# A weight's conversion in the token stage: the last addition done by an accumulating DMA inside SBUF instead of VectorE

## The chip, the cores and the metric

The kernel runs on one core of one Trainium2 chip. The metric is the device time of one execution in microseconds (us). A core has a matmul engine (TensorE, "PE" in the profile; "PEld" is its weight loads), three engines for elementwise work (VectorE "DVE", ScalarE "ACT", GpSimd "POOL") and 16 DMA engines. Each engine works through its instructions in order. DMAs are issued from the instruction streams of SyncE ("SP"), ACT or POOL; those of SP and ACT go through a hardware queue (q1 and q10 in the profile), those of POOL through a software queue (q0), for which POOL itself spends time on each issue.

## What is computed

Hashed attention on 4 x 8 heads, 768 tokens, head width 64; its output, as 4 batches of 768 tokens by 512 columns, goes through a token mixer and a channel mixer:

```python
xt = x.transpose(0, 2, 1)
h = np.maximum(xt @ w_tok1, 0.0) @ w_tok2          # 768 -> 256 -> 768, over tokens
u = x + h.transpose(0, 2, 1)
h2 = np.maximum(u @ w_ch1, 0.0) @ w_ch2            # 512 -> 1536 -> 512, over columns
return (u + h2).astype(np.float32)
```

The four weights arrive in float64 (a float32 array multiplied by a float64 scalar). The kernel sees each number as two 32-bit words, the low and the high one, and turns it into float32 on the chip. The weight of this case is `w_ch2`, 1536 x 512, "second channel weight" below.

## The kernel before

The kernel has three stages, and the order of the instructions on every engine is the order in which the program emits them. **Attention** (0 to about 297 us) keeps its result transposed in the tile `XT`, 4 blocks of 128 columns by 3072 tokens. The **token stage** (`tokens`, about 297 to 368 us) follows, then the **channel stage** (`channels`).

*The token stage.* For each batch b, `mix1(b)` multiplies `w_tok1` with the batch (24 matmuls of 512 columns in two output halves j, L1226), and ScalarE applies the relu (L1233) into `r1`. `left_sums(b)` makes four sums of `r1` on VectorE (L1249 to L1252), and `mix2(b, m)`, for the two halves m, does the second product by seven smaller matmul products instead of eight (L1266). Their results lie in four PSUM banks; ScalarE copies some out (`p1` first, L1271, then L1274, L1276, L1278), VectorE adds them up (L1281 to L1285) into one of three `places` (parts of the tile `second`, used in rotation: `(2*b + m + 1) % 3`), and an accumulating DMA issued from POOL (L1286) adds that place to `XT`. There are eight of these DMAs, two per batch. A `mix2` may write its place only when the DMA that read the place three turns earlier has landed. All PSUM results of the stage share eight banks in rotation. The order is: `mix1(0)`, the sums of the token weight (`weight_sums`, L1203 to L1206), `left_sums(0)`; then for b = 1, 2, 3: `mix1(b)`, `left_sums(b)`, `mix2(b-1, 0)`, `mix2(b-1, 1)`; at the end `mix2(3, 0)`, the first inputs of the channel stage (`inputs`, L1178 and L1179), `mix2(3, 1)`.

*The conversions.* Between these, at fixed places, `job()` takes the next entry of a list: first the sums of the first channel weight (L1316 to L1321), then eight times `conversion.one`, each for a piece of `w_ch2` of 128 partitions x 3 row blocks x 256 columns (768 numbers per partition). Calls of `job` stand after each half of `mix1` and between the two `mix2` of b = 1, 2, 3. So conversion 1 comes at the end of `mix1(0)`, conversions 2 and 3 in `mix1(1)`, 4 between `mix2(0, 0)` and `mix2(0, 1)`, 5 and 6 in `mix1(2)`, 7 between `mix2(1, 0)` and `mix2(1, 1)`, 8 in `mix1(3)`; `mix2(2, .)` and `mix2(3, .)` have none left.

`one` consists of four steps. `begin` lets ScalarE write |high word as float32| x 2^-112 into `size` (L177). `join` works on VectorE: L187 makes `unit`, the power of two that the number's exponent stands for, by shifting `size` and masking; L191 shifts `size` in place, which gives the absolute value cut to the bits of the high word; L195 multiplies the low word by 2^-52 and by `unit`; L196 adds this to `size`. `end` (L206, VectorE) puts the sign of the high word on the sum and writes it into `WC2`, the float32 weight. `fetch` (L169, SP) loads the next raw piece. `size` has two buffers, `raw` three, and `unit` one.

Of the kernel before, what the change touches and what calls it, by code (L numbers as in the profile page):

```python
# [36 lines left out]
F32 = mybir.dt.float32  # L37
BF16 = mybir.dt.bfloat16
U32 = mybir.dt.uint32
I32 = mybir.dt.int32  # L40
I64 = mybir.dt.int64
ALU = mybir.AluOpType
# [6 lines left out]
def kernel(  # L49
# [16 lines left out]
    nc = tc.nc  # L66
    P = 128
# [9 lines left out]
    NHT = DCH // P  # L77
# [56 lines left out]
    NW = 768  # L134
# [6 lines left out]
    class Conversion:  # L141


        def __init__(self, pool, parts, bufs):
            self.pool, self.bufs = pool, bufs
            self.todo = [
                (w, dst, rows, j, n)
                for w, dst, rows, blocks in parts
                for j in range(*blocks, rows)
                for n in range(0, dst.shape[2], NW // rows)  # L150
            ]
            self.fetched, self.begun, self.ready = [], None, None
            for _ in range(bufs - 1):
                self.fetch()
# [55 lines left out]
        def turnover(self):  # L210

            self.end()
            self.fetch()

        def one(self):

            self.begin()
            self.join()
            self.end()
            self.fetch()  # L220
# [1085 lines left out]
    def weight_sums(w, sums, first, second, low, high):  # L1306

        a00, a01 = w[:, first, low], w[:, second, low]
        a10, a11 = w[:, first, high], w[:, second, high]

        def early():
            nc.vector.tensor_tensor(sums[:, 1], a00, a10, op=ALU.subtract)  # L1316
            nc.vector.tensor_tensor(a10, a10, a11, op=ALU.add)

        def late():
            nc.vector.tensor_tensor(sums[:, 0], a10, a00, op=ALU.subtract)  # L1320
            nc.vector.tensor_tensor(sums[:, 2], a01, sums[:, 0], op=ALU.subtract)  # L1321

        return [early, late]

    def channels(pool, psum, SW1, second, TA, judge):
# [384 lines left out]
        def hidden_pair(s, t):  # L1710
# [5 lines left out]
            r, (p2, p6, p7, p3, p4) = parts_of(s, t)  # L1716
            p5, p1 = Smaller(None, "p5", s, t), ahead.pop()
            one, two, three, four = ring
            e2, e4, e5, e3 = [flat(output_at(i)) for i in ((2, 1, 1, 2) if t == 1 else (0, 1, 3, 2))]
            e6 = e7 = flat(q1)  # L1720
# [52 lines left out]
            p3.rest()  # L1773
            p3.unite()
            A = bank_pair(one)
            p4.one(A, e4)
            p7.seed()
# [23 lines left out]
            if t + 1 < GP:  # L1801
                later(t + 1, "p3", *bounds(r))
                later(t + 1, "end", lambda: relu(r[3]), lambda: relu(r[2]))
                open_next(two, s, t)
                if t == 1:
                    end_look()
                ring[:] = [two, three, one, four]
                postponed.append((direct, end))
            else:
                plus(r[1], banks(C), rows(e3))  # L1810
                unfinished.append(lambda: (relu(r[3]), [work() for work in bounds(r)]))
                ring[:] = [two, one, three, four]
                postponed.append((direct, lambda: (end(), relu(r[2]))))
# [402 lines left out]
    def inside(stage, *args):  # L2216
        with tc.tile_pool(name="sb", bufs=2, reuse_waits="tile") as pool, tc.tile_pool(
            name="ps", bufs=2, space=PSUM, reuse_waits="tile"
        ) as psum, tc.manual_schedule():
            stage(pool, psum, *args)  # L2220
# [10 lines left out]
    n = NHT // 4 * P  # L2231
# [10 lines left out]
    def attention_and_tokens(W1, W2, x0):  # L2242
        inside(attention, W1, W2, x0)
        pool = late.enter_context(tc.tile_pool(name="late", bufs=1, side="right", reuse_waits="tile"))
        SW1 = big["SW1"] = pool.tile([P, 3, NCB // 2, DCH // 2], F32, name="SW1")
        TA = big["TA"] = pool.tile([P, 2, NCB // 2, TT], F32, name="TA")
        n = NHT * DM

        def second_tile(i):
            return pool.tile([P, (n, n * 3 // 4)[i]], F32, name=f"second{i}", tag=f"second{i}", bufs=1)  # L2250

        WC2 = second["WC2"] = second_tile(0).rearrange("p (k c) -> p k c", k=NHT)
        second["SW2"] = second_tile(1).rearrange("p (i k c) -> p i k c", i=3, k=NHT // 2)
        second["tile"] = second_tile

        def weights(pool):
            return Conversion(pool, [(w_ch2, WC2, 3, (0, NHT))], bufs=3)

        def jobs(conversion):
            early, late = weight_sums(  # L2260
                WC1, SW1, slice(0, NCB // 2), slice(NCB // 2, NCB), slice(0, DCH // 2), slice(DCH // 2, DCH),
            )
            return [
                lambda: (early(), late()),
                *[conversion.one] * (NHT * DM // NW),
            ]

        SW2 = second["SW2"].rearrange("p i k c -> p i (k c)")
        places = [SW2[:, i] for i in range(3)]
        inside(tokens, W1, W2, x0, weights, jobs, [TA[:, 0], None, TA[:, 1], None], places)  # L2270
# [100 lines left out]
```

## Time and profile before

| | |
|---|---|
| runs shown | 766.54, 766.83, 766.92 us, median 766.83 |
| profiled execution | span 766.2 us from the first to the last instruction; its own execution time is not listed apart from the three runs |
| PE busy | 758.5 us, 99% of the span |
| DVE busy | 673.5 us, 88% |
| ACT, POOL busy | 442.4 us (58%), 189.7 us (25%) |
| accumulating DMAs of the token stage (L1286) | 8, of 768 KB each |
| pieces of `w_ch2` converted | 8, of 384 KB (float32) each |

In the profile, a group line reads: line, engine, operation, output<-input tiles, shapes, count | busy us, mean ns of one | idle time of the engine before them and what ended it. A timeline line reads: start in us, duration in us, engine, line, operation, tiles, count, and in brackets the idle time before it with its releaser; "<-issue" stands for a wait whose cause the profile doesn't show. `WC2` and the three `places` appear under the tile name `second`, `r1` as `r`, the token weights as `W`, PSUM banks of the stage as `t`. A line of a view by stretches gives the stretch in us, its length, then the busy time of each engine with its number of instructions, the granted TensorE clock, the busy share of the DMA engines and GB/s. The lines themselves stand in the prediction.

### The profile page before, as it was taken

The numbers are of one execution on the slowest core, as the hardware profiler recorded it, in microseconds if no ns is written. First come the engines' busy times: TensorE is split into PE (matmuls) and PEld (weight loads), VectorE is DVE, ScalarE is ACT, GpSimd is POOL, SyncE is SP. The second block draws the span as 40 slices with busy tenths as digits, with TensorE's granted clock in tenths as the row PEclk, the third lists the DMA queues.
The fourth block names the chain that finished last, engine by engine and source line by source line (L and its number), as shares of the span: only waits on it lengthen the run. The fifth ranks groups of instructions, "written<-read, shape, count | busy, mean of one in ns | idle before, by whom it ended". The sixth has DMA issues, their size and how long they took to land.

```text
span 766.2 us, 14575 instructions
## 1 busy us (share of the span) xinstructions
PE 758.5 (99%) x5549; PEld 509.8 (67%) x5549; DVE 673.5 (88%) x969; ACT 442.4 (58%) x816; POOL 189.7 (25%) x266
## 2 busy tenths in 40 slices
PE   9999999999999999999999999999999999999997
PEld 4565655666656554455444468888877888886886
DVE  5899899899997998999788798998899799889884
ACT  6677777677776873333232326566666667665331
POOL 2346771638761820011220100100000011000001
PEclk9999999999999999999999999999999999999999
DMA  7746587575965549876697997889576696750665
GB/s 257 271 172 184 179 240 225 181 179 186 217 202 116 168 68 254 310 178 119 112 321 244 348 360 263 244 233 277 171 220 210 234 261 140 235 157 8 207 157 130
DMA packets 131210, 157.80 MB, mean 206 GB/s; under 512 B 56000, under 2 KB 99520, under 8 KB 129216
## 3 DMA queue, kind: packets, MB, share of 16 engines
q1 hardware_dynamic: 119248, 136.05, 56.3%
q0 software_dynamic: 11600, 20.53, 13.1%
q8 instruction: 45, 0.74, 0.4%
q10 hardware_dynamic: 288, 0.25, 0.1%
q14 instruction: 29, 0.24, 0.1%
HBM read 107.71 MB, written 40.67 MB: 194 GB/s over the span
## 4 chain that ended last, share of the span: by engine, by line
PE 88%; DVE 8%; DMA 2%; issue 1%; SPq 0%; DVEq 0%; ACT 0%; ACTq 0%
PE b L1353 51%; PE sc L503 16%; PE acc L470 14%; PE sc L425 1%; PE hash L536 1%; PE ss L848 1%; DVE size L196 1%; PE sacc L874 1%; DVE unit L195 1%; DMA XT<-second 1%; DVE second L206 1%; PE hash L348 1%; DVE size L191 1%; PE ssums L862 1%; PE hash L353 1%
## 5 line engine op out<-in xcount | busy, mean ns | idle before, releaser
L414 ACT ACTIVATE exps<-sc 128x768 f32<-128x768 f32 (+1 forms) x181 | 126.5, 765 | 10.1 <-PE sc L503 7.2
L1353 PE MATMUL b<-R,second 128*128 128x256 f32 (+1 forms) x522 | 131.8, 408 | 0.0
L503 PE MATMUL sc<-qk 32*128 32x384 f32 (+1 forms) x1352 | 120.1, 457 | 0.0
L1353 PEld LDWEIGHTS b<-R,second 128*128 128x128 f32 x522 | 99.1, 190 | 28.5 <-issue 16.5
L470 PE MATMUL acc<-exps,vn 128*32 128x385 f32 (+1 forms) x1344 | 111.7, 486 | 0.0
L503 PEld LDWEIGHTS sc<-qk 32*128 32x128 f32 x1352 | 92.3, 185 | 16.9 <-issue 4.4
L1359 ACT COPY c<-b 128x256 f32<-128x256 f32 (+1 forms) x96 | 40.3, 426 | 79.3 <-PE b L1353 66.1
L470 PEld LDWEIGHTS acc<-exps,vn 128*32 128x32 f32 x1344 | 43.9, 109 | 62.0 <-issue 60.0
L376 POOL DMA_DIRECT2D bits<-XT x104 | 54.6, 526 | 72.1 <-DVE XT L366 27.4
L459 DVE TENSOR_TENSOR esd<-esd,exps 128x768 f32<-128x768 f32 x70 | 67.0, 957 | 4.3
L1353 PE MATMUL b<-XT,WC 128*128 128x256 f32 (+1 forms) x208 | 61.0, 428 | 0.0
L791 POOL DMA_INDIRECT table<-XT,sorting x48 | 57.1, 1190 | 14.7 <-issue 13.2
L2063 POOL DMA_DIRECT2D out<-second x7 | 8.5, 1213 | 187.3 <-DVE second L2057 81.5
L557 ACT COPY rec<-rec 32x384 f32<-32x384 f32 x56 | 28.5, 510 | 41.0 <-DVE rec L551 39.6
L1353 PEld LDWEIGHTS b<-XT,WC 128*128 128x128 f32 x208 | 39.5, 190 | 15.4 <-issue 10.3
L503 PE MATMUL sc<-bits 32*128 32x384 bf16 (+1 forms) x338 | 48.0, 311 | 0.0
L1353 PE MATMUL b<-XT,SW 128*128 128x256 f32 (+1 forms) x164 | 47.0, 410 | 0.0
L455 DVE TENSOR_TENSOR esd<-esd,exps 128x768 f32<-128x768 f32 x42 | 40.3, 958 | 4.4
L1226 PE MATMUL t<-x,W 128*128 128x512 f32 x96 | 42.1, 594 | 0.2 <-DMA x<-bounced 0.2
L1353 PEld LDWEIGHTS b<-XT,SW 128*128 128x128 f32 x164 | 31.1, 190 | 9.4 <-issue 4.1
L1286 POOL DMA_DIRECT2D XT<-second x8 | 9.9, 1233 | 95.8 <-DVE unit L187 56.2
L1226 PEld LDWEIGHTS t<-x,W 128*128 128x128 f32 x96 | 18.1, 190 | 23.3 <-issue 21.7
(333 smaller groups left out, 1455.9 us busy)
## 6 DMA issues: line engine op xcount, KB each, us to landing
second<-left SPq DMA_DIRECT2D x20, 768.0 KB
qk<-in_qk_rows SPq DMA_DIRECT2D x13, 1152.0 KB
raw<-in_moe_w_ch SPq DMA_DIRECT2D x16, 768.0 KB
second<-left SPq DMA_DIRECT2D x18, 576.0 KB
WC<-hidden_left SPq DMA_DIRECT2D x18, 448.0 KB
x<-bounced SPq DMA_DIRECT2D x4, 1536.0 KB
XT<-second POOLq DMA_DIRECT2D x8, 768.0 KB
seen<-in_qk SPq DMA_DIRECT2D x15, 384.0 KB
```

The source lines that it names most:

```text
L376: nc.gpsimd.dma_start(out=to[at : at + 2 * BITS, half[j]], in_=g[of : of + 2 * BITS])
L414: return nc.scalar.activation(e[:, :, columns], sc, ACT.Exp, scale=SCALE)
L455: nc.vector.tensor_tensor(self.d, self.d, e, op=ALU.add)
L459: nc.vector.tensor_tensor(self.d, self.d, e, op=ALU.add)
L470: made = nc.tensor.matmul(acc[D * i + d : D * i + d + 32], vn[:, i, c, d : d + 32], e[:, i], start=(c == 0), stop=(c == NR - 1),)
L503: nc.tensor.matmul(made[j, piece][:, i], k[at : at + 32, ks], q[at : at + 32], start=part < 0, stop=part == 1,)
L557: nc.scalar.copy(rec[other : other + 32, h], rec[at : at + 32, h])
L791: nc.gpsimd.indirect_dma_start(out=tables[2 * w + i], out_offset=bass.IndirectOffsetOnAxis(ap=self.at[:, x : x + 1], axis=0), in_=row, in_ ...
L1226: nc.tensor.matmul(ps, W1[:, r, P * j : P * j + P], x[:, r], start=(r == 0), stop=(r == NR - 1),)
L1286: nc.gpsimd.dma_start(out=XT[:, 2 * m : 2 * m + 2, S * b : S * b + S], in_=to.rearrange("p i n t -> p i (n t)"), accum_op=ALU.add,)
L1353: nc.tensor.matmul(ps, left(k), right(k), start=start and k == ks[0], stop=stop and k == ks[-1], skip_group_check=True,)
L1359: nc.scalar.copy(c, ps)
```

## The change

For the second channel weight alone, `one` calls a new step `signed` between `begin` and `join`; `join` and `end` then find nothing to do. `signed` shifts `size`, puts the sign of the high word on it and writes this into `WC2` directly (the high part of the number, with its sign); takes sign and exponent of that value with the mask 0xFF800000 into `unit`; multiplies the low word by 2^-52 and by `unit` (the low part, with its sign); and adds `unit` to `WC2` by a DMA issued from POOL that accumulates at its destination. Four VectorE instructions and one DMA stand in the place of five VectorE instructions. `unit` keeps its single buffer. The sum is the same; the rest of the kernel, and the conversions of the other three weights, stay as they are.

```diff
-        def __init__(self, pool, parts, bufs):
-            self.pool, self.bufs = pool, bufs
+        def __init__(self, pool, parts, bufs, summed=False):
+            self.pool, self.bufs, self.summed = pool, bufs, summed
...
+        def signed(self):
+
+            raw, size, to, rows = self.begun
+            self.begun = None
+            unit = self.pool.tile([P, NW], F32, name="unit", tag="unit", bufs=1)
+            lo, hi, size, part = (
+                a.rearrange("p (t n) -> p t n", t=rows) for a in (raw[:, :, 0], raw[:, :, 1], size.bitcast(U32), unit)
+            )
+            bits = to.bitcast(U32)
+            nc.vector.tensor_scalar(size, size, 3, None, op0=ALU.logical_shift_left)
+            nc.vector.scalar_tensor_tensor(
+                bits, hi, 0x80000000, size, op0=ALU.bitwise_and, op1=ALU.bitwise_or,
+            )
+            nc.vector.tensor_scalar(part.bitcast(U32), bits, 0xFF800000, None, op0=ALU.bitwise_and)
+            nc.vector.scalar_tensor_tensor(part, lo, 2.0**-52, part, op0=ALU.mult, op1=ALU.mult)
+            nc.gpsimd.dma_start(out=to, in_=part, accum_op=ALU.add)
+
         def one(self):
 
             self.begin()
+            if self.summed and self.begun:
+                self.signed()
             self.join()
             self.end()
             self.fetch()
...
-            return Conversion(pool, [(w_ch2, WC2, 3, (0, NHT))], bufs=3)
+            return Conversion(pool, [(w_ch2, WC2, 3, (0, NHT))], bufs=3, summed=True)
```

## The prediction

> **What bounds the kernel now.** I read the page's first part, then the stretches of the token stage, where the eight conversions lie, then the timelines of POOL, DVE and ACT there.
>
> ```profile
> span 766.2 us, 14575 instructions
> PE 758.5 (99%) x5549; PEld 509.8 (67%) x5549; DVE 673.5 (88%) x969; ACT 442.4 (58%) x816; POOL 189.7 (25%) x266
> ```
>
> ```profile
> core 0: us, PE busy (x) PEld busy (x) DVE busy (x) ACT busy (x) POOL busy (x), PEclk, DMA share, GB/s
> 310.00:320.00 10.00, 10.00 (x31) 5.45 (x30) 9.69 (x16) 5.74 (x11) 0.00 (x0) 1.00 0.77 281
> 330.00:340.00 10.00, 10.00 (x32) 5.79 (x31) 9.69 (x15) 5.94 (x11) 1.27 (x1) 1.00 0.96 200
> 350.00:360.00 10.00, 10.00 (x33) 5.89 (x32) 9.48 (x18) 4.33 (x10) 2.42 (x2) 1.00 0.44 79
> 360.00:370.00 10.00, 9.91 (x30) 5.30 (x29) 9.24 (x16) 3.15 (x7) 1.22 (x1) 1.00 0.76 135
> ```
>
> DVE is nearly full (9.2 to 9.7 of 10), but PE is full: 10.00 of 10.00. DVE lags behind PE and the PSUM banks absorb the lag. So DVE time freed here buys nothing by itself; all of PE's idle time in these rows is the 0.09 us in the last. The end of the kernel moves only if PE is made to wait. The place where PE is nearest to waiting is the last `mix2`:
>
> ```profile
> 365.07 0.48 ACT L1271 COPY second<-t 128x384 f32<-128x384 f32 x1 [2.91 <-DMA XT<-second]
> 365.60 0.30 PEld L1266 LDWEIGHTS t<-W2sums,r1s 128*128 128x128 f32 x2 [0.70 <-ACT second L1271]
> ```
>
> ACT waits 2.91 us there for an accumulating DMA that still reads the place `mix2(3, 1)` wants, and the PE side for ACT. With three places in rotation that is the DMA of `mix2(2, 0)`, the fifth of eight. POOL's timeline shows how they follow each other:
>
> ```profile
> 324.99 1.35 POOL L1286 DMA_DIRECT2D XT<-second  x1 [50.63 <-DVE unit L187]
> 332.61 1.27 POOL L1286 DMA_DIRECT2D XT<-second  x1 [6.27 <-ACT second L1274]
> 343.68 1.20 POOL L1286 DMA_DIRECT2D XT<-second  x1 [9.79 <-DVE second L1285]
> 350.46 1.22 POOL L1286 DMA_DIRECT2D XT<-second  x1 [5.58 <-DVE unit L187]
> 358.57 1.20 POOL L1286 DMA_DIRECT2D XT<-second  x1 [6.89 <-DVE second L1285]
> 365.30 1.22 POOL L1286 DMA_DIRECT2D XT<-second  x1 [5.53 <-issue]
> 372.05 1.20 POOL L1286 DMA_DIRECT2D XT<-second  x1 [5.53 <-DVE TB L1183]
> 378.80 1.21 POOL L1286 DMA_DIRECT2D XT<-second  x1 [5.55 <-DVE seen L1859]
> ```
>
> The last four start 6.73, 6.75 and 6.75 us apart, each after 5.5 us of idle POOL, under three different named releasers, none of which the DMA's data needs. The fifth landed at 365.07 (ACT's wait ends) and POOL starts the sixth at 365.30. I read this as: of DMAs this large, POOL's queue has one in flight, and the next issue waits until it has landed. Small ones do go out closely:
>
> ```profile
> 62.47 1.27 POOL L791 DMA_INDIRECT table<-XT,sorting  x1 [0.38 <-issue]
> 63.74 0.53 POOL L376 DMA_DIRECT2D bits<-XT  x1
> ```
>
> So it is room for descriptors rather than a rule of one at a time. By the code an `XT` DMA has 256 pieces (128 partitions x 2 runs of 3 KB). The new one has 384 (128 x 3 runs of 1 KB at its destination). If two of 256 don't fit together, 256 beside 384 don't either.
>
> **The change part by part.** VectorE's part, from the groups of DVE in the token stage:
>
> ```profile
> L206 DVE SCALAR_TENSOR_TENSOR second<-raw,size 128x768 uint32<-128x768 uint32 x8 | 7.7, 958 | 0.3
> L196 DVE TENSOR_TENSOR size<-size,unit 128x768 f32<-128x768 f32 x8 | 7.7, 958 | 0.3
> L195 DVE SCALAR_TENSOR_TENSOR unit<-raw,unit 128x768 f32<-128x768 uint32 x8 | 7.6, 951 | 0.0
> L191 DVE TENSOR_SCALAR size<-size 128x768 uint32<-128x768 uint32 x8 | 4.5, 560 | 0.3
> L187 DVE TENSOR_SCALAR unit<-size 128x768 uint32<-128x768 uint32 x8 | 4.4, 552 | 0.0
> ```
>
> `signed` keeps one shift (as L191), one sign step (as L206), one mask (as L187) and one multiply (as L195) and drops L196: 8 x 0.96 = 7.7 us of DVE, hidden behind PE. One conversion falls from 3.9 us to 2.95 us: 1.55 to the end of the sign step, 1.4 for the mask and the multiply.
>
> What is added is eight DMAs of 384 KB on POOL's queue. No accumulating DMA of this shape is in the trace, so I build its cycle (issue to next possible issue) from the one that is:
>
> ```profile
> q0 software_dynamic: 272, 0.79, 65.6%
> XT<-second POOLq DMA_DIRECT2D x8, 768.0 KB
> 508.03 0.61 POOL L2170 DMA_DIRECT2D seen<-in_qk  x1 [6.09 <-ACT seen L2160]
> ```
>
> The first line is the DMA queues' view of 365.30 to 372.05 us, when this queue alone ran: 65.6% of 6.75 = 4.4 us of data. Issue takes 1.2 us, and 1.15 us are left for start and landing. For the new DMA: data by bytes 2.2 us; start and landing 1.15; issue 1.8, since 128 pieces take 0.61 us (last line; the 128 from the code) and 256 take 1.2. Together C = 5.2 us. From below it costs half of the row, 3.4 us, if pieces cost nothing at issue and all else goes by bytes. From above, if small pieces move slowly:
>
> ```profile
> q0 software_dynamic: 207, 0.42, 45.1%
> ```
>
> This is 492 to 498 us, a DMA in 2 KB pieces (beside other traffic): 45.1% of 6 us x 16 engines / 207 = 0.21 us a piece, against 0.26 us for 3 KB (65.6% of 6.75 x 16 / 272). On that line 1 KB costs 0.16 us; times 24 per engine, 3.8 us of data, C = 6.8. I take 5.2: of the two rows the first, an accumulation inside SBUF without other traffic, is the nearer.
>
> The Trainium skill ("DMA: Bandwidth & Descriptors", section "Anatomy of one DMA — SWDGE (gpsimd) path") puts a POOL-issued DMA at about 2.0 us plus its bytes at 436 GB/s; an estimate by it is 2.9 us for the new DMA. For the `XT` DMA it gives 3.8 us, where this trace has 6.5 (358.57 to 365.07), so the trace does not agree for accumulating ones. By the page's C the delay worked out below would be about 5 us in place of 21.
>
> Two new waits come with it. First, the `XT` DMAs queue behind the new ones on POOL, and the `places` behind them. Second, `unit` has one buffer: the mask of conversion n+1 on DVE waits until DMA n has landed, and behind it on DVE wait `left_sums` and the additions of `mix2`, which free PSUM banks and feed PE. Now the schedule, with M = 6.73 for an `XT` DMA (landing 0.2 us before the next issue, as above; C likewise), from these starts on DVE:
>
> ```profile
> 304.48 0.56 DVE L187 TENSOR_SCALAR unit<-size 128x768 uint32<-128x768 uint32 x1
> 308.47 0.55 DVE L1203 TENSOR_TENSOR W2sums<-W 128x384 f32<-128x384 f32 x1
> 310.46 0.42 DVE L1249 TENSOR_TENSOR TA<-r 128x256 f32<-128x256 f32 x1
> 312.18 0.55 DVE L187 TENSOR_SCALAR unit<-size 128x768 uint32<-128x768 uint32 x1
> 321.73 0.55 DVE L1281 TENSOR_TENSOR second<-t,second 128x384 f32<-128x384 f32 x1
> 324.38 0.55 DVE L187 TENSOR_SCALAR unit<-size 128x768 uint32<-128x768 uint32 x1
> 338.78 0.42 DVE L1249 TENSOR_TENSOR TA<-r 128x256 f32<-128x256 f32 x1
> ```
>
> They give weight sums 1.99, `left_sums` 1.72 and one `mix2` 2.65 us on DVE.
>
> - Conversion 1 ends at 304.48 + 2.95 = 307.4; its DMA lands at 312.4. Conversion 2 starts at 307.4 + 1.99 + 1.72 = 311.1, needs `unit` at 312.7: free. It ends at 314.1; its DMA lands at 319.1.
> - Conversion 3 follows at once, needs `unit` at 315.6 and waits 3.5 us; it ends at 320.5. C3 is issued 320.5, POOL free 325.7.
> - `mix2(0, 0)` is done on DVE at 320.5 + 1.72 + 2.65 = 324.9; its DMA goes 325.7 to 332.4. C4 to 337.6. The DMA of `mix2(0, 1)` to 344.4. Conversion 5 had to wait for C4 and ended at 338.8, so C5 is next, lands 349.4; POOL free 349.6.
> - Conversion 6 waits for that landing, ends 350.8 (before: 338.8, the last row above). C6 to 356.0, `mix2(1, 0)` to 362.7, C7 to 367.9, `mix2(1, 1)` to 374.6, C8 to 379.8.
> - The DMA of `mix2(2, 0)` then starts at 379.8 in place of 358.57, and lands 6.5 us later, at 386.3 in place of 365.07.
>
> **Late by 21.2 us**, at the very wait that ends last today. PE waits earlier too (`mix1(3)` needs a bank that `mix2(1, 0)`, now over 10 us late, frees), but this is inside the same delay. After 386.3 everything follows as before, since today's order also hangs on that landing: the three remaining DMAs 6.75 us apart, and POOL's addition L1397 behind them.
>
> Two small terms. The first `XT` DMA took 7.62 us to the second's issue (324.99 to 332.61) where a later one took 6.73, beside loads; such loads run beside the new DMAs too: +0.9. And PE, after some 7 us of waiting, restarts cold:
>
> ```profile
> 3.99 1.95 PE L388 MATMUL opening<-qk,projs 128*32 128x384 f32 x8 [0.34 <-DMA qk<-in_qk]
> 8.31 0.85 PE L388 MATMUL opening<-qk,projs 128*32 128x384 f32 x8
> ```
>
> The same eight matmuls took 1.1 us longer at the start of the kernel: +1.1, bounded by 0 and 2.2 (twice that). The Trainium skill ("TensorE: Matmul & The Clock Gate", Part 1) has the clock at half after about 3.4 us of idleness, for about 3.4 us of work; this would be an estimated +1.7 in place of +1.1.
>
> Sum: 21.2 + 0.9 + 1.1 = 23.2. The profiled execution has a span of 766.2; the runs' median is 766.8, 0.6 more, so 766.8 + 23.2 = **790.0 us**. C enters seven times (C2 before conversion 3, and C3 to C8): 3.4 gives 23.2 - 12.6 = 10.6, or 777; 6.8 gives 23.2 + 11.2 = 34.4, or 801.
>
> **The rivals.**
>
> *Room for two.* A new DMA and an `XT` DMA fit in flight together. Then only the waits for `unit` are left: conversion 3 ends at 320.5, conversion 6 waits from 335.0 for C5's landing at 338.5 and ends at 339.9, 1.1 later than before; `mix1(3)` on PE
>
> ```profile
> 338.93 10.46 PE L1226 MATMUL t<-x,W 128*128 128x512 f32 x24
> ```
>
> needs `mix2(1, 0)`'s bank only for its second half, at 344.1, and has it at about 342. The DMA of `mix2(2, 0)` shares engines with C8 (2.2 us of data) and lands up to 3 us later: about 768.5. For it: small DMAs overlap. Against it: the four 5.5 us gaps.
>
> *Not slower: the new DMAs fill POOL's gaps.* POOL is idle 50.6, 6.3 and 9.8 us before the first three `XT` DMAs. If a cycle were at or below 5.2 - 21.2 / 7 = 2.2 us, the fifth `XT` DMA would not land later, and DVE's 7.7 us would stay as a gain; PE can use no more than the 0.09 us at 365, plus what it waits at the stage's start: 766.5. Against it: half of the measured cycle is already 3.4.
>
> *Dearer DMAs.* The 384 pieces don't fit the queue's room in one go, or each costs as much as a 3 KB one (24 x 0.26 = 6.2 us of data, C = 9.2): 28 us more, about 818.
>
> *It doesn't do what it says*, if the weight arrived in float32: L206 on `second` runs eight times, so the conversion is there.
>
> **How the numbers follow.** The forecast, one large DMA in flight, 0.76; room for two 0.12 (half of it within 0.2%); filled gaps 0.05; dearer DMAs 0.07. 0.2%, 1.5 us, is about what a measurement of this kernel can tell from no change. Faster 0.02, same 0.10, slower 0.88. The range is the forecast's own, by C's bounds, a little wider below for its other terms: 775 to 802; it leaves out the rivals and little else.
>
> **What would show it.** POOL's timeline: new DMAs and `XT` DMAs strictly one after another, 5 to 7 us apart, without gaps from 320 us on. DVE: idle before the mask of conversions 3, 5 and 6, ended by a DMA `second<-unit`. PE: a wait of some 10 us in `mix1(3)`, and one in `mix2(3, 1)` that ends with the landing of the fifth `XT` DMA near 387. Channel stage: same length. Wrong if POOL issues a new DMA beside one in flight, if C is far from 5.2 us, or if PE stays full up to 365.

## The result and the profile after

The changed kernel takes 808.12 us (807.66 to 808.48, 4 runs) against 766.88 us before: a ratio of 1.0539, 95% interval 1.0526 to 1.0552, 41.2 us slower. The forecast was 790.0 with a range of 775 to 802: the sign and the places of the waits were right, the size was not. The page of the kernel after, first lines:

```profile
span 806.7 us, 14607 instructions
PE 768.9 (95%) x5549; PEld 510.3 (63%) x5549; DVE 667.7 (83%) x961; ACT 442.5 (55%) x816; POOL 199.4 (25%) x274
```

PE was 99% busy and is 95% busy now. The view by stretches, for the token stage alone (from its first matmul to the first one of the channel stage), first of the kernel before, then of the kernel after; behind the length stand the busy times of PE, PEld, DVE, ACT and POOL, the granted clock, the DMA share and GB/s:

```profile
289.12:367.64 78.52, 78.21 (x212) 39.32 (x209) 73.07 (x112) 28.69 (x53) 7.46 (x6) 1.00 0.80 211
```

```profile
287.80:407.46 119.66, 89.39 (x212) 43.35 (x209) 69.71 (x104) 28.51 (x53) 17.83 (x14) 0.87 0.73 168
```

The stage grew from 78.5 to 119.7 us, 41.1 us, which is the whole loss. PE does the same matmuls in it, but waits about 30 us (119.66 - 89.39) and is busy 11 us longer at a granted clock of 0.87. POOL's timeline of the kernel after (L230 are the new DMAs, L1305 the `XT` DMAs, up to the fifth):

```profile
307.63 1.44 POOL L230 DMA_DIRECT2D second<-unit  x1 [34.58 <-DMA raw<-in_moe_w_ch]
318.98 1.35 POOL L230 DMA_DIRECT2D second<-unit  x1 [9.91 <-DVE size L224]
332.31 1.29 POOL L230 DMA_DIRECT2D second<-unit  x1 [11.98 <-DVE r1s L1268]
339.67 1.21 POOL L1305 DMA_DIRECT2D XT<-second  x1 [6.06 <-issue]
347.35 1.29 POOL L230 DMA_DIRECT2D second<-unit  x1 [6.47 <-issue]
352.30 1.22 POOL L1305 DMA_DIRECT2D XT<-second  x1 [3.65 <-issue]
360.24 1.29 POOL L230 DMA_DIRECT2D second<-unit  x1 [6.72 <-issue]
367.32 1.29 POOL L230 DMA_DIRECT2D second<-unit  x1 [5.79 <-DVE TA L1268]
372.93 1.20 POOL L1305 DMA_DIRECT2D XT<-second  x1 [4.32 <-DVE second L225]
379.70 1.30 POOL L230 DMA_DIRECT2D second<-unit  x1 [5.57 <-DVE second L225]
384.62 1.21 POOL L1305 DMA_DIRECT2D XT<-second  x1 [3.62 <-issue]
391.41 1.30 POOL L230 DMA_DIRECT2D second<-unit  x1 [5.58 <-DVE second L1300]
396.39 1.21 POOL L1305 DMA_DIRECT2D XT<-second  x1 [3.67 <-DVE second L1304]
```

From 339.67 on they go strictly one after another: a new DMA holds the queue for 4.95, 4.92 and 4.98 us (347.35, 379.70 and 391.41 to the next start), an `XT` DMA for 6.78 when alone. The masks on DVE that wait for the one `unit` buffer, from DVE's timeline of the kernel after:

```profile
316.56 0.95 DVE L228 TENSOR_SCALAR unit<-second 128x768 uint32<-128x768 uint32 x1 [4.69 <-DMA second<-unit]
329.93 0.95 DVE L228 TENSOR_SCALAR unit<-second 128x768 uint32<-128x768 uint32 x1 [9.96 <-DMA second<-unit]
339.45 0.95 DVE L228 TENSOR_SCALAR unit<-second 128x768 uint32<-128x768 uint32 x1 [1.75 <-DMA second<-unit]
352.13 0.95 DVE L228 TENSOR_SCALAR unit<-second 128x768 uint32<-128x768 uint32 x1 [6.62 <-DMA second<-unit]
364.96 0.95 DVE L228 TENSOR_SCALAR unit<-second 128x768 uint32<-128x768 uint32 x1 [9.43 <-DMA second<-unit]
...
384.45 0.95 DVE L228 TENSOR_SCALAR unit<-second 128x768 uint32<-128x768 uint32 x1 [5.62 <-DMA second<-unit]
```

These six waits come to 38 us. A mask's start marks a landing: the first three new DMAs landed 8.9, 11.0 and 7.1 us after their issue (316.56 - 307.63, 329.93 - 318.98, 339.45 - 332.31), where the forecast had 5.0 for each. And PE, with the copy it waited for last:

```profile
334.11 7.17 PE L1245 MATMUL t<-x,W 128*128 128x512 f32 x12 [9.22 <-DVE second L1300]
369.15 8.41 PE L1245 MATMUL t<-x,W 128*128 128x512 f32 x12 [9.21 <-DVE second L1300]
403.47 1.65 PE L1285 MATMUL t<-W2sums,r1s 128*128 128x384 f32 x2 [5.71 <-ACT second L1290]
...
407.46 4.54 PE L1372 MATMUL b<-XT,WC 128*128 128x512 f32 x8
411.84 1.88 PE L1372 MATMUL b<-TA,WC 128*128 128x512 f32 x4
```

```profile
402.93 0.48 ACT L1290 COPY second<-t 128x384 f32<-128x384 f32 x1 [8.53 <-DMA XT<-second]
```

PE waits twice for a PSUM bank that DVE, held up at a mask, frees late (second halves of `mix1(2)` and `mix1(3)`), for shorter times besides (2.6 us at most), and at last in `mix2(3, 1)` for the place that the fifth `XT` DMA reads. That landed at 402.93 in place of 365.07: 37.9 us of the 41.2.

### The profile page after: what moved, and what is told of

The parts are those of the page before. It is cut to its first block, busy times and chain, and to the rows that moved or that the text cites. A ratio compares the mean times of both kernels' runs of the same rounds, so it can differ in the third digit from the quotient of the medians.

```text
span 806.7 us, 14607 instructions
## 1 busy us (share of the span) xinstructions
PE 768.9 (95%) x5549; PEld 510.3 (63%) x5549; DVE 667.7 (83%) x961; ACT 442.5 (55%) x816; POOL 199.4 (25%) x274
## 4 chain that ended last, share of the span: by engine, by line
PE 81%; issue 9%; DVE 3%; DMA 3%; POOL 2%; ACT 1%; SPq 0%; POOLq 0%; DVEq 0%; ACTq 0%
PE b L1372 49%; PE sc L522 14%; PE acc L489 12%; PE sc L444 1%; PE hash L555 1%; DMA second<-unit 1%; PE ss L867 1%; POOL second L230 1%; PE sacc L893 1%; DMA XT<-second 1%; DMA bounced<-second 1%; POOL XT L1305 1%; PE ssums L881 1%; PE hash L367 1%; PE t L1285 1%
## 5 line engine op out<-in xcount | busy, mean ns | idle before, releaser
L522 PEld LDWEIGHTS sc<-qk 32*128 32x128 f32 x1352 | 90.5, 185 | 19.5 <-issue 5.9
L1245 PE MATMUL t<-x,W 128*128 128x512 f32 x96 | 47.5, 651 | 18.6 <-DVE second L1300 18.4
L810 POOL DMA_INDIRECT table<-XT,sorting x48 | 56.8, 1182 | 14.7 <-issue 14.4
L1245 PEld LDWEIGHTS t<-x,W 128*128 128x128 f32 x96 | 19.9, 211 | 45.7 <-issue 24.3
L228 DVE TENSOR_SCALAR unit<-second 128x768 uint32<-128x768 uint32 x8 | 7.6, 953 | 38.1 <-DMA second<-unit 38.1
```

The lines of the kernel that those rows point to most:

```text
L522: nc.tensor.matmul(made[j, piece][:, i], k[at : at + 32, ks], q[at : at + 32], start=part < 0, stop=part == 1,)
L810: nc.gpsimd.indirect_dma_start(out=tables[2 * w + i], out_offset=bass.IndirectOffsetOnAxis(ap=self.at[:, x : x + 1], axis=0), in_=row, in_ ...
L1245: nc.tensor.matmul(ps, W1[:, r, P * j : P * j + P], x[:, r], start=(r == 0), stop=(r == NR - 1),)
```

## The experiments

All times are medians beside runs of the kernel before on the same chip; the ratio is to those, with its 95% interval.

**Without the DMA.**

```diff
-            nc.gpsimd.dma_start(out=to, in_=part, accum_op=ALU.add)
```

> The new four VectorE instructions stay, the accumulating DMA is left out, so the low parts of the second channel weight are never added (they are left out of the result). Theory (the DMAs on POOL's queue cost it all, VectorE's relief is worth nothing because PE is full): the time of before, 766.8 us within 0.5. Rival (some of the loss lies in the new VectorE instructions, whose mask takes 0.95 us in place of 0.55): above 768. Rival (the relief of VectorE does buy something): below 765.

766.19 us against 766.44, ratio 0.9998 (0.9988 to 1.0007), within the expectation when it is counted from this chip's 766.44. The four VectorE instructions, with the mask at 0.95 us in place of 0.55, cost nothing, and the relief they bring buys nothing. All of the loss comes with the DMA, that is with its place in POOL's queue and with the wait for `unit`, which went with it.

**Without the loads beside the first DMAs.**

```diff
-            raw = self.pool.tile([P, NW, 2], U32, name="raw", tag="raw", bufs=self.bufs)
-            nc.sync.dma_start(out=raw.rearrange("p (t n) w -> p t (n w)", t=rows), in_=src)
+            if self.summed and len(self.todo) < NHT * DM // NW - 2:
+                raw = self.last
+            else:
+                raw = self.last = self.pool.tile([P, NW, 2], U32, name="raw", tag="raw", bufs=self.bufs)
+                nc.sync.dma_start(out=raw.rearrange("p (t n) w -> p t (n w)", t=rows), in_=src)
...
-            if not turned and b + 2 < B:
-                fetch(b + 2, x)
```

> The changed kernel, but without the loads that run beside the first new DMAs: the token stage loads no batch 2 and 3 (batches 0 and 1 are used again) and only three of eight raw pieces of the second channel weight (the third is converted again for the rest), so that weight and the token mixing of two batches are wrong parts of the computation. Theory (what the forecast missed is that the first three new DMAs take 8.9, 11.0 and 7.1 us because loads of the hardware queue are ahead of them): each new DMA lands about 4.9 us after its issue, and the time falls by 14 to 17 us to 791 to 794, near the forecast of 790. Rival (the new DMAs are slow there for another reason, such as VectorE's work beside them or the first use of the queue): 805 or more.

793.28 us, ratio 1.0343 (1.0326 to 1.036), 26.8 above before, as expected: of the loss of 41.2 us, 14.4 are gone. POOL's timeline of this kernel, where the new DMA is L233 and the `XT` DMA L1306:

```profile
307.89 1.44 POOL L233 DMA_DIRECT2D second<-unit  x1 [34.58 <-DVE W2sums L1225]
315.24 1.35 POOL L233 DMA_DIRECT2D second<-unit  x1 [5.91 <-DVE size L227]
322.43 1.29 POOL L233 DMA_DIRECT2D second<-unit  x1 [5.84 <-DVE r1s L1269]
327.37 1.21 POOL L1306 DMA_DIRECT2D XT<-second  x1 [3.65 <-DVE size L227]
...
382.27 1.21 POOL L1306 DMA_DIRECT2D XT<-second  x1 [3.67 <-DVE second L1304]
```

The third new DMA frees the queue after 4.94 us, the first `XT` DMA starts at 327.37 in place of 339.67, and the fifth at 382.27 (forecast for the changed kernel: 379.8). The fifth landed at 388.80, by the copy that waited for it:

```profile
388.80 0.48 ACT L1291 COPY second<-t 128x384 f32<-128x384 f32 x1 [8.47 <-DMA XT<-second]
```

That is 14.1 us before the 402.93 of the changed kernel. With the loads gone, the forecast's schedule is nearly what happens. (The kernel before was not run without these loads; its PE is full, so they can hardly cost it time.)

**Without the loads of two batches alone.** The last part of that diff, with all raw pieces loaded.

> The changed kernel without the loads of batches 2 and 3 (batches 0 and 1 are mixed again, so half of the result is wrong), with all raw pieces loaded. Theory (the second new DMA took 11 us because the load of batch 3, 1.5 MB issued 1.2 us before POOL had finished issuing it, was ahead of it on the DMA engines; the raw pieces, half as large, cost about half): the second new DMA lands about 7 us after its issue, the first XT DMA starts 4 to 7 us earlier than in the changed kernel, and the time is 795 to 801, between 793.3 without all these loads and 808. Rival (the raw pieces alone were the delay): 806 or more.

800.37 us, ratio 1.0431 (1.0413 to 1.0448), 33.2 above the kernel before on this chip (767.15). The time is within the expectation. The second new DMA, issued at 316.03, landed at 322.34, 6.3 us later in place of 11.0, and the first `XT` DMA started at 331.38, 8.3 us earlier than in the changed kernel, where 4 to 7 were expected. The batch loads account for somewhat over half of what all these loads cost (8.0 of 14.4 us); the rest goes to the raw pieces by difference, as no run leaves out these alone. What the DMA meets is seen in the DMA engines' view of the changed kernel, first from 320.4 (POOL has just issued the second new DMA) to 323.9, then from 324.4 to 329.5; the columns are packets, MB and share of 16 engines:

```profile
q1 hardware_dynamic: 515, 1.02, 86.1%
```

```profile
q1 hardware_dynamic: 560, 1.13, 63.1%
q0 software_dynamic: 399, 0.39, 47.7%
```

For 3.5 us the engines serve the hardware queue alone and not one packet of POOL's; then both share them. In the kernel without all these loads, from the issue of the second new DMA (315.24) to 317.24, POOL's queue has moved its first packets:

```profile
q0 software_dynamic: 9, 0.01, 3.0%
```

There it begins within 2.0 us of the issue; in the changed kernel it has not begun 4.9 us after it (318.98 to 323.9). That the loads are the cause is shown by leaving them out; by which rule the engines took the loads first stays open.

**More room for descriptors, kernel before and kernel after.**

```diff
-                self.d = pool.tile([P, 2, HALF], F32, name="esd", tag="esd", bufs=4)
+                self.d = pool.tile([P, 2, HALF], F32, name="esd", tag="esd", bufs=3)
...
-        "TRN2", target_bir_lowering=False, num_devices=1, dynamic_dma_scratch_size=1024
+        "TRN2", target_bir_lowering=False, num_devices=1, dynamic_dma_scratch_size=2048
```

(Two small constants of the attention stage moved into its own pool as well, to free the space.)

> The kernel before with twice the room for descriptors of POOL's DMAs (2048 in place of 1024 bytes a partition; the space comes from one of four buffers of a tile of the attention stage, and from two small constants that now live in that stage only). Theory (POOL holds back an issue because two large accumulating DMAs don't fit into the descriptors' room): the starts 6.73 to 6.75 us apart at the end of the token stage move together to 2 to 4 us, as VectorE gets ready; the time stays 766.8 within 2, as PE is full (the buffer taken away may cost something in attention). Rival (POOL's queue has one large DMA in flight whatever the room): still 6.7 us apart.

> The changed kernel with twice the room for descriptors of POOL's DMAs, from the same space. Theory (half of the loss is the XT DMAs queueing behind the new ones for room, the rest VectorE waiting for the one unit buffer): the XT DMAs start when VectorE is ready; the fifth lands near 386 in place of 402.9, and the time is about 791, 785 to 797. Rival (the wait for unit alone sets the pace): above 800. Rival (the room alone does): below 775.

Before with more room: 768.87 us, ratio 1.0029 (1.0016 to 1.0042), 2.4 us above the kernel before on the same chip, a little more than the 2 allowed. The fifth, sixth and seventh `XT` DMAs of its timeline:

```profile
359.57 1.19 POOL L1291 DMA_DIRECT2D XT<-second  x1 [6.98 <-DVE second L1290]
362.51 1.22 POOL L1291 DMA_DIRECT2D XT<-second  x1 [1.75 <-ACT second L1281]
365.24 1.20 POOL L1291 DMA_DIRECT2D XT<-second  x1 [1.51 <-DVE second L1290]
```

They start 2.9 and 2.7 us apart in place of 6.7, as VectorE gets ready, and the time does not fall by it. So it was the room that held them back, not a rule of one at a time. After with more room: 791.29 us, ratio 1.0329 (1.0309 to 1.0349), as expected, with the fifth `XT` DMA landing at 387.73. In its timeline an `XT` DMA starts 2.6 us behind a new one:

```profile
343.35 1.29 POOL L230 DMA_DIRECT2D second<-unit  x1 [3.75 <-DVE unit L229]
345.95 1.21 POOL L1310 DMA_DIRECT2D XT<-second  x1 [1.31 <-DVE second L1309]
```

**A second place for `unit`.**

```diff
-            unit = self.pool.tile([P, NW], F32, name="unit", tag="unit", bufs=1)
+            self.turn = not getattr(self, "turn", False)
+            if self.turn:
+                unit = big["TA"][:, 1].rearrange("p k t -> p (k t)")[:, :NW]
+            else:
+                unit = self.pool.tile([P, NW], F32, name="unit", tag="unit", bufs=1)
```

> The changed kernel with a second place for unit (every other conversion uses a part of TA that is free until the inputs of the channel stage), so a mask waits for the DMA of the conversion two before it. Theory (room for descriptors on POOL's queue sets the pace and VectorE's wait adds gaps to it): VectorE's waits for unit fall from 38 us to under 12, but the new and the XT DMAs still go one after another, some 78 us from the first issue to the fifth XT DMA's issue, which then lands near 392 in place of 402.9: about 797, 793 to 801. Rival (the wait for unit alone was the loss): under 775.

799.15 us, ratio 1.0413 (1.0396 to 1.0431). VectorE's waits for the two places come to 17 us together (12.2 and 5.2) in place of 38, more than the 12 expected; the time is the expected one, and the fifth `XT` DMA landed at 393.65. The rival, that this wait alone is the loss, falls.

**Both waits eased.** The second place and the larger room together.

> Both waits eased at once: the second place for unit, and twice the room for descriptors of POOL's DMAs. Theory (these two waits are the whole loss, and the DMAs' data beside other traffic costs nothing by itself): the XT DMAs start within 3 us of their times before, PE stays full, and the time is that of the kernel before with the larger room, 768.9, within 3. Rival (a third cost, such as the DMA engines being shared): above 775.

773.44 us, ratio 1.0073 (1.0056 to 1.009). That misses the expectation (765.9 to 771.9), and stays below the rival's 775: the time alone does not decide. Counted from the kernel before on its own chip, this kernel loses 6.3 us and the kernel before with the larger room 2.4, so 3.9 lie between them. By the view of stretches, the token stages of the kernel before with more room and of this kernel:

```profile
289.80:368.70 78.90, 78.23 (x212) 39.29 (x209) 73.34 (x112) 28.59 (x53) 8.63 (x7) 1.00 0.83 216
```

```profile
296.01:375.64 79.63, 78.17 (x213) 39.38 (x210) 68.26 (x101) 27.86 (x52) 19.23 (x15) 1.00 1.06 252
```

The token stage takes 79.6 us against 78.9: here the two waits are the whole loss but for 0.7 us, though the DMA share is 1.06. The loads still slow a new DMA: the second, issued at 320.89, landed at 332.24, 11.4 us later. So with the two waits eased, a late landing costs next to nothing here. The rest lies ahead of the stage (296.0 against 289.8), where the two kernels have the same code. This profiled execution took 775.62 us, the longest of the four; the kernel after with more room, again with the same code there, began its token stage at 291.35. Why attention was longer in this execution stays open.

**Fewer pieces.**

```diff
-            nc.gpsimd.dma_start(out=to, in_=part, accum_op=ALU.add)
+            nc.gpsimd.dma_start(out=size.bitcast(F32), in_=part, accum_op=ALU.add)
```

> The changed kernel, but the new DMA adds the low part to the buffer size (128 runs of 3 KB at its destination) in place of the weight (384 runs of 1 KB), so the low parts are left out of the weight. Theory (pieces cost at issue, and each waits its turn beside the loads; the data phase goes by bytes): POOL issues it in about 0.6 us in place of 1.3, a new DMA without other traffic cycles in 4.2 us in place of 4.95, and with six of them in the chain the time falls by 4 to 8 us, to 800 to 804. Rival (pieces cost nothing beyond their bytes): 807 or more. Rival (pieces are most of the cost): under 797.

789.98 us, ratio 1.0298 (1.0281 to 1.0316): 18 us less than the change, at the same bytes. More was gained than expected; by the time alone this is the rival, that pieces are most of the cost. POOL issues it in about 0.9 us, not 0.6. The expectation and its rivals saw only a shorter cycle; the timeline shows something else:

```profile
342.36 0.90 POOL L230 DMA_DIRECT2D size<-unit  x1 [4.15 <-ACT size L177]
344.78 1.22 POOL L1305 DMA_DIRECT2D XT<-second  x1 [1.52 <-DVE second L1304]
```

An `XT` DMA starts 2.4 us behind the new one, in the old room. By the code that is 128 + 256 pieces; 384 + 256 and 256 + 256 don't go together. As 128 and 384 pieces are the same bytes here, the room is counted in pieces. This time is close to the one with doubled room (791.29), as it should be if the effect is the same. (The edit also makes ScalarE wait for the landing before it may write `size` again, up to 9.0 us at 330.16; so the gain comes in spite of a new wait.)

**One DMA alone.**

```diff
-            if self.summed and self.begun:
+            if self.summed and self.begun and not self.todo and not self.fetched:
```

> Only the eighth conversion uses the new step and its DMA, the first seven stay as they were. Theory (a new DMA costs its place in POOL's queue): it stands between the fourth and the fifth XT DMA, is issued when the fourth has landed, near 357.2, and frees POOL 4.95 us later; the fifth XT DMA starts near 362.2 in place of 358.6 and PE waits about 3.6 us more for its landing: 770.4, 769.5 to 772 (up to a microsecond of it for a cold start of PE). Rival (one DMA alone hides in the slack, the loss needs the series of eight): 767.0 or less.

772.69 us against 767.91, ratio 1.0064 (1.0048 to 1.0079): 4.8 us slower (3.7 to 6.1). The expectation has 769.5 to 772, or 2.7 to 5.2 over 766.8: the time lies 0.7 above it, the loss against the kernel before on this chip within it. The queue did what was expected:

```profile
349.10 1.22 POOL L1305 DMA_DIRECT2D XT<-second  x1 [5.58 <-DVE size L224]
355.89 1.29 POOL L230 DMA_DIRECT2D second<-unit  x1 [5.58 <-PE t L1285]
360.88 1.23 POOL L1305 DMA_DIRECT2D XT<-second  x1 [3.69 <-DVE second L1301]
```

The new DMA held POOL for 4.99 us. The rest is PE's restart, in its timeline:

```profile
367.97 1.65 PE L1285 MATMUL t<-W2sums,r1s 128*128 128x384 f32 x2 [3.82 <-ACT second L1290]
```

PE waited 3.82 us, and from there to the first matmul of the channel stage it took 4.0 us (371.97) for what took 2.04 before (365.60 to 367.64), where the expectation allowed a microsecond.

## Why the prediction was wrong in size

- **PE is the bound, VectorE's time buys nothing**: right, shown by the kernel without the DMA. VectorE's busy time fell by 5.8 us (673.5 to 667.7), not 7.7: the mask takes 0.95 us, where the forecast took L187's 0.55 for it.
- **One large DMA in flight, for want of room**: right, shown by the larger room in both kernels, and by the DMA in fewer pieces.
- **C = 5.2 us for a new DMA**: right where nothing else runs (4.92 to 4.98). Its issue cost 1.3 us, not 1.8. By the Trainium skill ("DMA: Bandwidth & Descriptors", "Anatomy of one DMA — SWDGE (gpsimd) path") it would be an estimated 2.9 us; the trace, with 4.9, does not agree.
- **Conversions 3, 5 and 6 wait for `unit`**: right, and conversions 2, 4 and 8 waited too.
- **The fifth `XT` DMA sets the end**: right. It landed 37.9 us late, not 22.1 (21.2 and the 0.9 for loads).
- **"Such loads run beside the new DMAs too: +0.9"** is the step that failed. The forecast took it from one `XT` DMA, whose issue fell at the end of a load, and counted it once. The first three new DMAs are issued while loads are waiting on the engines, and took 27.0 us to land (8.9, 11.0 and 7.1) in place of 15.0: 12.0 us where the sum has 0.9. Conversions 2 and 3 wait for the first two of these landings, and the first `XT` DMA for the third. The forecast's own rows gave a warning, a DMA share of 0.77 from 310 to 320 us and of 0.96 from 330 to 340. Against the forecast's schedule, the third was issued 11.8 us late (332.3 against 320.5), the first `XT` DMA started 14.0 us late (339.7 against 325.7), the fifth 16.6 (396.4 against 379.8). Leaving the loads out took 14.4 us off the loss, 1.2 of it by a shorter restart of PE (1.7 us in place of the 2.9 below).
- **"+1.1, bounded by 0 and 2.2" for PE's restart** was also too small. It came from the kernel's first matmuls, at which the view by stretches of the kernel before has a granted clock of 1.00 (3.99 to 6.00 us), so that row did not show the clock. In the changed kernel the six products after the last wait took 3.99 us (403.47 to 407.46) against 2.04 before (365.60 to 367.64), and the next eight matmuls 4.38 (to 411.84) against 3.43, by PE's timeline of the kernel before: 2.9 us.

```profile
367.64 3.60 PE L1353 MATMUL b<-XT,WC 128*128 128x512 f32 x8
371.07 1.88 PE L1353 MATMUL b<-TA,WC 128*128 128x512 f32 x4
```

Put together: 37.9 + 2.9 = 40.8, and the spans differ by 40.5.

Of the rivals, "room for two" is what one gets by making the room. "Dearer DMAs" had the time nearest to the result (818) for a wrong reason: the pieces were not dearer, and the DMA was not split.

## What to carry to other kernels

Before work is moved from an engine to POOL's DMA queue, ask what else stands in that queue, who waits for it, and whether two such DMAs fit in it together; the room goes by pieces, so one contiguous run per partition may be worth more than the bytes say. A buffer that such a DMA reads is busy until the landing, so with one buffer the next producer waits for a whole DMA. And price a DMA beside the loads that run at its issue, not alone: here 5 us became up to 11.

## What the runs showed of the hardware

A DMA from POOL that was issued behind loads of the hardware queue had no packet served for 3.5 us in which the engines worked for that queue, and the first three such DMAs landed 7 to 11 us after their issue in place of 5. So the two queues did not share the engines evenly from the start.

With the room of 1024, POOL issued no second such DMA beside one in flight when the two together had, by the code, 512 or 640 pieces, and did with 384; with 2048 it did with 512 and 640.

PE's clock falls to half after a wait, but the length of the wait alone does not decide it. In the token stages of these runs half a clock followed every wait of 3.35 us or more, and none of up to 1.88. In between both are seen. In the changed kernel four matmuls took 2.80 us after a wait of 2.11 us, and 1.45 where the clock was full:

```profile
388.70 2.80 PE L1285 MATMUL t<-W,r 128*128 128x384 f32 x4 [2.11 <-DVE second L1300]
395.01 1.45 PE L1285 MATMUL t<-W,r 128*128 128x384 f32 x4
```

The kernel without the batch loads kept a granted clock of 1.00 after 2.70 us (380.32 to 386), and stood at 0.50 from the first matmul after a wait of 3.65 (342.71).

The fall can also come after PE has resumed. In the kernel with fewer pieces, after a wait of 2.57 us, the first pair of matmuls still took 0.91 us, and a pair of the same size 1.4 us later took 1.47:

```profile
350.82 0.91 PE L1285 MATMUL t<-W2sums,r1s 128*128 128x384 f32 x2 [2.57 <-ACT second L1290]
...
352.22 1.47 PE L1285 MATMUL t<-W2sums,r 128*128 128x384 f32 x2
```

After the wait that counts in the changed kernel, the granted clock from 403.47 to 407.46 is 0.50:

```profile
403.47:407.46 3.99, 3.99 (x6) 2.18 (x7) 1.65 (x3) 1.19 (x3) 0.91 (x1) 0.50 0.70 122
```

The Trainium skill ("TensorE: Matmul & The Clock Gate", Part 1) puts both the idle time that halves the clock and the work that restores it at about 3.4 us. The trace does not agree with the first as a bound, with half a clock after 2.11 us. By the second the restart costs an estimated 1.7 us; the one that counts here cost 2.9, and the one in the kernel without all the loads 1.7 (389.33 to 396.49, which took 5.47 before).
